# A fused attention and gated MLP kernel: fewer PSUM banks for the direct gelu tiles, and other places for the exps that VectorE computes

## The chip, the cores and the metric

The kernel runs on one core of one Trainium2 chip. The metric is the device time of one execution in microseconds; the time before is the median of four runs, 462.97 us (462.76 to 463.13). Engines are named as in the profile: PE is TensorE's matmul (PEld its weight load), DVE is VectorE, ACT is ScalarE, POOL is GpSimd, SP is the engine that issues most DMAs.

## What is computed

The reference normalises `x` (2048 rows of 448), sends the result through a 16-head attention with head size 28 and, beside it, through an MLP with gelu and silu, and combines both with `x`. Cut to what matters:

```
xn = layernorm(x)                                  # [2048, 448]
q, k, v = split(xn @ wqkv)                         # 16 heads of 28
o = softmax(q k^T / sqrt(28)) v                    # per head, 2048 x 2048 scores
s = o @ wo
h = gelu_tanh(xn @ w1 + b1)                        # [2048, 1792]
g = silu(h @ w2 + b2)                              # [2048, 448]
return x + s * g
```

## The kernel before

**Tiles.** Everything is done on transposed data. The 2048 rows are four chunks `c` of 512, the 16 heads four groups `g` of four. A score tile is 128 keys by 512 queries of one head; there are 4 x 4 blocks of 16 x 4 tiles, 1024 in all, numbered `m`. PE computes a tile from `kT` and `qT` with 32 active rows, so that up to four tiles of different heads run in the array at once. An exp follows (without a maximum; the norms of q and k that are folded into one row keep it in range), and PE multiplies the result by `vaug` and sums in the PSUM bank `acc` (PV, four heads side by side in columns).

**Who does the exps.** Most are done by ACT, in units of two or three tiles straight from PSUM (`p_exps`, L1276). The 33 quads of four tiles that `QUADS` lists are done by DVE instead: one pass from PSUM per tile, here called a head (`p_apass`, L1379), and then five passes over all four tiles in SBUF (`p_expq`, L1430 to L1437). So 132 tiles are DVE's, and 892 are ACT's.

**PSUM.** Of eight banks, `acc` holds the PV sum, six are the `ring`, and the last is `misc`. ACT's units alternate between ring banks 0 to 2 (three tiles) and banks 4 and 5 (two tiles). Ring bank 3 and `misc` are the side banks. All other products that need a bank, projections, w1 and w2 products, head tiles, normalisation and output products, take one from the list `banks` and give it back (`bank()` takes the one that came free first).

**The order of the work.** A planner in the kernel writes each engine's program. It runs small processes (generators) that yield tasks with a planned duration and a priority, or wait for a condition or a bank; it always takes the task that can start first, within 0.1 us the one with the lowest priority number. PE executes its program in order, and waits in it for semaphores of ACT and DVE. A head tile waits until it can join the pending ring score of other heads (`may_join`, `join`), for at most `WAIT`; during gelu it is issued alone at once (`in_gelu`). A quad may start when the scores have come to its first tile, during gelu up to `GLEAD` = 32 tiles earlier (`p_late`). Where the planned share of PE over 3.4 us falls under 85%, `p_busy` inserts fillers, three products with a zero matrix into `acc` (L903).

**Gelu.** The gelu of all 56 tiles of h (128 x 512 each) is done in one stretch, as ACT must load another table for it. 35 tiles were computed earlier and copied to SBUF by DVE (`p_f1`, L1070); ACT applies gelu to these in pieces of 5, 5, 4, 5, 5, 4, 5 and 2. Between the pieces come seven groups of three tiles which ACT reads directly from PSUM (`DIRECT`, `p_direct`, `p_gelu`, L1125). During this stretch the ring holds no scores: the direct groups use all six banks, in turns of three. For that, `p_take3` takes bank 3 from the list, from twelve tiles before `GM` until the last direct group is read, and DVE's heads have `misc` alone. The stretch begins with the first unit whose last tile is at or beyond `GM` = 582 (`gu` is its number). The score of unit `gu + 1` is issued when the last direct group is read.

**Where the exps' results lie.** ACT writes into 18 slots of `P`, before gelu also into 9 + 12 slots in the still unused parts of `h`, and after gelu into 15 slots of `xnT`, which is not read any more (`p_room`, `assign`; the profile's names for outputs are therefore P, h and xnT). `room_free` holds gelu's direct pieces until the slots in `h` are read by PV.

**After gelu** come the w2 products (`p_f2`, L1146), the silu of each chunk (a tanh on ACT, `p_silu`, L1161), the normalisation of each block (`p_epi`) and the output products (`p_out`, `p_last`).

Of the kernel before, what the change touches and what calls it, by code (L numbers as in the profile page):

```python
# [24 lines left out]
NRING = 6  # L25
NP = 18
# [1 line left out]
MTOT = NBLK * T * 4  # L28

GM = 64 * 9 + 6  # L30
QUADS = (17, 22, 24, 35, 36, 50, 55, 66, 75, 85, 89, 97, 106, 116, 118, 132, 139, 147, 148, 149, 151, 163, 173, 178, 186, 193, 201, 209, 216, 222, 225, 235, 242)
SM_SCALE = DH ** -0.5
LOG2E = 1.4426950408889634
EXP_A3, EXP_A2, EXP_LC = 0.16391228, 0.00783292, 1.1187538523466403
# [14 lines left out]


# [23 lines left out]
class _Kernel:  # L74
# [183 lines left out]
    def alloc(self):  # L258
# [3 lines left out]
        B = _Buf  # L262
# [104 lines left out]
        self.b_P += self.b_hf[2][5:14] + self.b_hf[3][0:12] + [B() for _ in range(16)]  # L367
        self.pon = [(0, NP)]
        self.b_nm = [[B(), B()] for _ in range(C)]
        self.b_selb = B()  # L370
# [13 lines left out]
    def schedule(self):  # L384
        K = self
# [695 lines left out]
    def t_f1(self, c, ft, bank, tok, k, prio=5):  # L1081
# [7 lines left out]
            return ins  # L1089
        return _Task(PE, f, [K.b_w1, K.b_w1pad, K.b_xnT[c][k]], [tok], 0.432, 0.17, prio)  # L1090

    def p_direct(self):
        K = self
        yield ("until", lambda: K.gu is not None and K.exp_u >= K.gu - 1 and K.bank3)
        s0 = 3 * ((K.gu - 1) % 2)
        for i, (c, f0) in enumerate(DIRECT):
            b0 = (s0 + 3 * i) % NRING
            yield ("until", lambda: K.exp_u >= K.gu - 1 + i if i < 2 else K.dir_read >= i - 1)
            for n in range(3):
                for k in range(2):  # L1100
                    yield K.t_f1(c, f0 + n, K.ring[:, b0 + n, :], K.b_ring[b0 + n], k, 3.5)
            K.dir_n += 1

    def p_gelu(self):
        K = self
        yield ("until", lambda: K.gu is not None and K.exp_u >= K.gu and K.n_f1 == len(SBT))
        left = [FT] * C
        s0 = 3 * ((K.gu - 1) % 2)
        for q, pc in enumerate(PIECES):
            if pc:  # L1110
                c, f0, n = pc
                src = K.h[:, c, 512 * f0:512 * (f0 + n)]
                rd = []
            else:
                i = K.dir_read
                yield ("until", lambda: K.dir_n > i and K.room_free())
                (c, f0), n = DIRECT[i], 3
                b0 = (s0 + 3 * i) % NRING
                src = K.ring[:, b0:b0 + 3, :].rearrange("p b n -> p (b n)")
                rd = K.b_ring[b0:b0 + 3]  # L1120
                for ft in range(f0, f0 + 3):
                    K.hf_free(c, ft)
            dst = K.h[:, c, 512 * f0:512 * (f0 + n)]
            left[c] -= n
            yield _Task(ACT, lambda eng, dst=dst, src=src: eng.activation(dst, src, ACTF.Gelu_apprx_tanh), rd,  # L1125
                        K.b_hf[c][f0:f0 + n] + ([K.b_h[c]] if left[c] == 0 else []),
                        0.4267 * n + (0.1 if pc else 0.06) + (1.3 if q == 0 else 0), 0.05, -1)
            if not pc:
                K.dir_read += 1
        K.prog[ACT].append(lambda eng: eng.preload_act_table_set("exp_and_others"))  # L1130
        K.tE[ACT] += 1.3
        for b in K.b_fsb + K.b_sig:
            b.w = K.b_w1.w
            b.r = list(K.b_w1.r) + [K.b_w1pad.w] + K.b_w1pad.r
        K.gelu_done = True

    def p_f2(self, c, t):
        K = self
        bank, tok = yield ("bank", lambda: K.b_h[c].tw is not None and K.ready([K.b_h[c], K.b_w2]) and K.dir_read == len(DIRECT) and (c < 2 or K.g_done[c - 2]))
        hv = K.h[:, c, :].rearrange("p (f n) -> p f n", n=512)  # L1140
        ps = bank[:, 0:D]
        for q in range(7):
            def f(eng, q=q):
                ins = None
                for ft in (2 * q, 2 * q + 1):
                    ins = eng.matmul(ps, hv[:, ft, t * 128:(t + 1) * 128], K.w2[:, ft, :],  # L1146
                                     start=(ft == 0), stop=(ft == FT - 1))
# [60 lines left out]
    def t_score(self, ms, bank_of, tok_of, prio):  # L1208
        K = self
        fl, rd = [], []  # L1210
# [22 lines left out]
    def p_scores(self):  # L1233
        K = self
        u = 0
        while K.next_m < MTOT:
# [1 line left out]
            if K.next_m >= MTOT:  # L1238
                break
            if K.gu is not None and u == K.gu + 1:  # L1240
                yield ("until", lambda: K.dir_read == len(DIRECT))
            b0 = 4 * (u % 2)
            n = 2 if b0 or K.next_m < 64 else 3
            if n == 3 and not K.taken:
# [99 lines left out]
        p["task"].dur, p["task"].rows = t.dur, t.rows  # L1344

    def in_gelu(self):
        return self.gu is not None and self.exp_u >= self.gu - 1 and self.dir_read < len(DIRECT)

    def p_late(self):
        K = self  # L1350
# [34 lines left out]
    def p_room(self):  # L1385
        K = self
        yield ("until", lambda: K.stg_done == 2)
        for ft in range(12):
# [5 lines left out]
        for b in K.b_P[NP + 21:]:  # L1394
            for x in K.b_xnT:
                for y in x:
                    b.r += y.r
        K.pon.append((NP + 21, 15))

    def room_free(self):  # L1400
        K = self
        return all(K.pv_done[m] for i, m in K.plast.items() if NP <= i < NP + 21)

    def assign(self, ms, b0):
        K = self
# [274 lines left out]
```

## Time and profile before

| | |
|---|---|
| median of 4 runs | 462.97 us |
| profiled execution | 463.12 us, of which the span from the first to the last instruction is 461.3 us |
| granted TensorE clock, mean | 0.996 |
| ACT busy | 448.1 us, 97% of the span |
| PE busy | 433.8 us, 94% |
| DVE busy | 368.2 us, 80% |
| POOL busy | 45.4 us, 10% |
| exps on ACT from the ring (L1276) | 363 instructions, 419.6 us (durations overlap) |
| direct gelus from the ring (L1125) | 7 instructions, mean 1457 ns |
| fillers on PE (L903) | 513 matmuls |

The profile shows one execution; its own time stands a little above the median. A row "busy" is the time in which the engine has at least one instruction in work. ACT overlaps the end of one instruction with the start of the next, so the distance from start to start (1.33 us for three tiles, 0.91 for two) is less than the duration in the groups. Idle time is put down to what ended it.

### The profile page before, as it was taken

The numbers are of one execution on the slowest core, as the hardware profiler recorded it, in microseconds if no ns is written. First come the engines' busy times: TensorE is split into PE (matmuls) and PEld (weight loads), VectorE is DVE, ScalarE is ACT, GpSimd is POOL, SyncE is SP. The second block draws the span as 40 slices with busy tenths as digits, with TensorE's granted clock in tenths as the row PEclk, the third lists the DMA queues.
The fourth block names the chain that finished last, engine by engine and source line by source line (L and its number), as shares of the span: only waits on it lengthen the run. The fifth ranks groups of instructions, "written<-read, shape, count | busy, mean of one in ns | idle before, by whom it ended". The sixth has DMA issues, their size and how long they took to land.

```text
span 461.3 us, 10748 instructions
## 1 busy us (share of the span) xinstructions
PE 433.8 (94%) x4509; PEld 169.1 (37%) x4543; DVE 368.2 (80%) x576; ACT 448.1 (97%) x407; POOL 45.4 (10%) x85
## 2 busy tenths in 40 slices
PE   6999899999999999999999999999999999999995
PEld 4533333333332233333333443233323344343552
DVE  7956898898887899968888577666877898996965
ACT  6999999999999999999999999999999999999994
POOL 7470000001010100000000000000000101101211
PEclk9999999999999999999999999999999999999998
DMA  8701000000000000000040000000000010200331
GB/s 266 269 2 37 2 1 0 1 2 3 2 1 1 1 0 3 2 1 2 1 141 0 1 3 0 2 2 1 0 1 1 1 41 2 35 9 1 43 43 41
DMA packets 8049, 11.17 MB, mean 24 GB/s; under 512 B 1697, under 2 KB 6993, under 8 KB 7954
## 3 DMA queue, kind: packets, MB, share of 16 engines
q1 hardware_dynamic: 6850, 8.43, 5.9%
q0 software_dynamic: 864, 1.38, 2.3%
q8 instruction: 36, 0.59, 0.5%
q10 hardware_dynamic: 288, 0.69, 0.4%
q14 instruction: 11, 0.09, 0.1%
HBM read 8.61 MB, written 3.21 MB: 26 GB/s over the span
## 4 chain that ended last, share of the span: by engine, by line
PE 48%; ACT 36%; issue 11%; DVE 2%; DMA 1%; SPq 0%; POOL 0%; ACTq 0%; DVEq 0%; POOLq 0%
ACT P L1276 18%; PE ring L1220 14%; ACT h L1276 10%; PE acc L1491 10%; ACT xnT L1276 6%; PE misc L1146 5%; PE ring L1146 4%; PE ring L1087 3%; PE acc L903 3%; PE misc L742 2%; PE misc L1087 2%; ACT h L1125 2%; PE ring L742 1%; DMA h<-in_A_wqkv_dram 1%; PE misc L1220 1%
## 5 line engine op out<-in xcount | busy, mean ns | idle before, releaser
L1276 ACT ACTIVATE P<-ring 128x1024 bf16<-128x1024 f32 (+1 forms) x194 | 221.8, 1260 | 1.8 <-PE misc L1220 0.8
L1220 PE MATMUL ring<-qT,kT 32*128 32x512 bf16 (+2 forms) x1082 | 142.6, 358 | 12.4 <-ACT P L1276 4.8
L1276 ACT ACTIVATE h<-ring 128x1024 bf16<-128x1024 f32 (+1 forms) x97 | 114.3, 1292 | 0.3 <-PE misc L1220 0.2
L1220 PEld LDWEIGHTS ring<-qT,kT 32*128 32x128 bf16 x1082 | 36.9, 91 | 133.3 <-ACT P L1276 57.5
L1276 ACT ACTIVATE xnT<-ring 128x1536 bf16<-128x1536 f32 (+1 forms) x72 | 83.5, 1269 | 0.0
L1491 PE MATMUL acc<-P,vaug 128*32 128x512 bf16 (+2 forms) x535 | 47.3, 358 | 0.0
L1561 POOL CAST rhi<-rc 128x16 bf16<-128x16 f32 x15 | 7.8, 523 | 359.2 <-DVE rc L1559 266.9
L903 PE MATMUL acc<-ident,zero 128*128 128x128 bf16 x513 | 41.4, 220 | 0.0
L1087 PE MATMUL ring<-xnT,w 128*128 128x512 bf16 x132 | 35.1, 381 | 1.5 <-issue 1.0
L903 PEld LDWEIGHTS acc<-ident,zero 128*128 128x128 bf16 x513 | 29.2, 98 | 17.6 <-issue 16.5
L1379 DVE TENSOR_SCALAR x_sb<-misc 128x512 uint16<-128x512 f32 x29 | 20.0, 689 | 13.0 <-PE misc L1220 12.9
L1146 PE MATMUL misc<-w,h 128*128 128x448 bf16 x112 | 27.2, 355 | 0.0
L1220 PE MATMUL misc<-qT,kT 32*128 32x512 bf16 (+1 forms) x70 | 26.0, 376 | 0.3 <-DVE qT L1578 0.3
L1146 PE MATMUL ring<-w,h 128*128 128x448 bf16 x112 | 26.0, 355 | 0.0
L1491 PE MATMUL acc<-h,vaug 128*32 128x512 bf16 x241 | 25.4, 384 | 0.0
L1087 PE MATMUL misc<-xnT,w 128*128 128x512 bf16 x70 | 20.0, 381 | 1.3 <-issue 0.5
L1491 PE MATMUL acc<-xnT,vaug 128*32 128x512 bf16 (+2 forms) x240 | 17.8, 330 | 0.4 <-ACT xnT L1276 0.4
L1491 PEld LDWEIGHTS acc<-P,vaug 128*32 128x32 bf16 x535 | 12.0, 95 | 14.7 <-issue 11.3
L1087 PEld LDWEIGHTS ring<-xnT,w 128*128 128x128 bf16 x144 | 11.3, 97 | 16.5 <-issue 5.3
L1379 DVE TENSOR_SCALAR x_sb<-ring 128x512 uint16<-128x512 f32 x19 | 13.0, 687 | 4.6 <-PE ring L1220 4.4
L1125 ACT ACTIVATE h<-h 128x2560 bf16<-128x2560 bf16 (+2 forms) x8 | 16.7, 2083 | 0.0
L1070 DVE CAST h<-misc 128x512 bf16<-128x512 f32 x20 | 13.7, 687 | 2.5 <-PE misc L1087 2.3
(270 smaller groups left out, 651.1 us busy)
## 6 DMA issues: line engine op xcount, KB each, us to landing
w<-in_B_w_dram SPq DMA_DIRECT2D x1, 1568.0 KB, 7.2
w<-in_B_w_dram SPq DMA_DIRECT2D x1, 1344.0 KB, 9.2
out_dram<-in_A_x_dram SPq DMA_DIRECT2D x3, 448.0 KB, 11.2
out_dram<-h POOLq DMA_DIRECT2D x6, 224.0 KB, 3.8
x_sb<-in_A_x_dram SPq DMA_DIRECT2D x2, 448.0 KB, 5.1
h<-in_A_wqkv_dram SPq DMA_DIRECT2D x3, 168.0 KB, 4.9
x_sb<-in_A_x_dram ACTq DMA_DIRECT2D x1, 448.0 KB, 5.3
h<-in_A_x_dram SPq DMA_DIRECT2D x1, 448.0 KB, 3.4
```

The source lines that it names most:

```text
L742: ins = eng.matmul(bank, w[:, kt, g * 128:(g + 1) * 128], K.xnT[:, kt, c * 512:(c + 1) * 512], start=(kt == 0), stop=(kt == KT - 1))
L903: ins = eng.matmul(K.acc[:, 0:128], K.zero[:, :], K.ident[:, :], start=False, stop=True, skip_group_check=True)
L1070: yield _Task(DVE, lambda eng: eng.tensor_copy(dst, bank), [tok], wr, 0.69, 0.0, 2)
L1087: ins = eng.matmul(bank, K.w1[:, kt, ft * 128:(ft + 1) * 128], K.xnT[:, kt, c * 512:(c + 1) * 512], start=(kt == 0), stop=(kt == KT - 1))
L1125: yield _Task(ACT, lambda eng, dst=dst, src=src: eng.activation(dst, src, ACTF.Gelu_apprx_tanh), rd, K.b_hf[c][f0:f0 + n] + ([K.b_h[c]] if ...
L1146: ins = eng.matmul(ps, hv[:, ft, t * 128:(t + 1) * 128], K.w2[:, ft, :], start=(ft == 0), stop=(ft == FT - 1))
L1220: return eng.matmul(dst, K.kT[32 * j:32 * j + 32, g, t * 128:(t + 1) * 128], K.qT[32 * j:32 * j + 32, g, c * 512 + q0:c * 512 + q0 + nq], ...
L1276: return eng.activation(reg[:, i0:i0 + n, :], K.ring[:, b0:b0 + n, :], ACTF.Exp, scale=SM_SCALE)
L1379: yield _Task(DVE, lambda eng: eng.tensor_scalar(K.unit[u][:, 512 * k:512 * k + 512].bitcast(dt.uint16), bank, SM_SCALE * LOG2E * 128.0, ( ...
L1491: return eng.matmul(K.acc[32 * j:32 * j + 32, q0:q0 + nq], K.vaug[:, t, 4 * g + j, :], ap[:, col:col + nq], tile_position=(0, 32 * j), sta ...
L1561: yield _Task(POOL, lambda eng: eng.tensor_copy(K.rhi[:, :], K.rc[:, :]), [K.b_rc], [K.b_rhl], 1.1, 0.0, 1)
```

## The change

The direct tiles of gelu no longer use all six ring banks. `directs()` forms eight groups (`ND`) in the ring's usual places, three tiles on banks 0 to 2 and two on banks 4 and 5 in turn, 20 tiles in all; the first group goes to the banks of unit `gu - 1`. Bank 3 is not taken from the list any more (`p_take3` is gone). 36 tiles go through SBUF now, in pieces of 5, 5, 4, 5, 5, 4, 4 and 4, each followed by a direct group, also the last. The slots for exps in `h` become 10 + 10 instead of 9 + 12. During gelu a quad may start up to 48 tiles early instead of 32. `QUADS` is another list of again 33 quads. The planner makes new orders for PE, DVE and ACT from all this.

```diff
-QUADS = (17, 22, 24, 35, 36, 50, 55, 66, 75, 85, 89, 97, 106, 116, 118, 132, 139, 147, 148, 149, 151, 163, 173, 178, 186, 193, 201, 209, 216, 222, 225, 235, 242)
+QUADS = (17, 22, 25, 35, 36, 50, 54, 65, 76, 84, 89, 99, 102, 116, 118, 132, 140, 142, 145, 152, 153, 162, 164, 179, 186, 194, 204, 210, 211, 214, 228, 233, 243)
...
-DIRECT = [(2, 5), (2, 8), (2, 11), (3, 0), (3, 3), (3, 6), (3, 9)]
+ND = 8
 PIECES = [(0, 0, 5), None, (0, 5, 5), None, (0, 10, 4), None, (1, 0, 5), None, (1, 5, 5), None, (1, 10, 4), None,
-          (2, 0, 5), None, (3, 12, 2)]
+          (2, 0, 4), None, (3, 10, 4), None]
...
-LEAD, WAIT, GLEAD = 0, 3.0, 32
+LEAD, WAIT, GLEAD = 0, 3.0, 48
...
-        self.pslots += [(hx(2, 5, 9), k) for k in range(9)] + [(hx(3, 0, 12), k) for k in range(12)]
+        self.pslots += [(hx(c, f, 10), k) for c, f in ((2, 4), (3, 0)) for k in range(10)]
...
-        K.spawn(K.p_take3(), 0)
...
+    def directs(self):
+        K = self
+        out, left = [], [[2, 4], [3, 0]]
+        for i in range(ND):
+            b0 = 4 * ((K.gu - 1 + i) % 2)
+            n = 2 if b0 else 3
+            c, f0 = left[i // (ND // 2)]
+            left[i // (ND // 2)][1] += n
+            out.append((c, f0, n, b0))
+        return out
...
     def p_direct(self):
         K = self
-        yield ("until", lambda: K.gu is not None and K.exp_u >= K.gu - 1 and K.bank3)
-        s0 = 3 * ((K.gu - 1) % 2)
-        for i, (c, f0) in enumerate(DIRECT):
-            b0 = (s0 + 3 * i) % NRING
+        yield ("until", lambda: K.gu is not None and K.exp_u >= K.gu - 1)
+        for i, (c, f0, nf, b0) in enumerate(K.directs()):
             yield ("until", lambda: K.exp_u >= K.gu - 1 + i if i < 2 else K.dir_read >= i - 1)
-            for n in range(3):
+            for n in range(nf):
...
-    def p_take3(self):
-        K = self
-        K.bank3 = False
-        yield ("until", lambda: K.next_m >= GM - 12 and any(t is K.b_ring[3] for _, t in K.banks))
-        e = K.banks.pop([t is K.b_ring[3] for _, t in K.banks].index(True))
-        K.bank3 = True
-        yield ("until", lambda: K.dir_read == len(DIRECT))
-        K.banks.append(e)
...
-        K.pon += [(NP, 9), (NP + 9, 12)]
+        K.pon += [(NP, 10), (NP + 10, 10)]
...
-        K.pon.append((NP + 21, 15))
+        K.pon.append((NP + 20, 15))
```

More of the change, by code (lines that the diff above doesn't have):

```diff
@@ L364, in alloc @@
         self.pslots = [(self.P[:, i0:i0 + n, :], k) for i0, n in ((0, NP),) for k in range(n)]
-        self.pslots += [(hx(2, 5, 9), k) for k in range(9)] + [(hx(3, 0, 12), k) for k in range(12)]
+        self.pslots += [(hx(c, f, 10), k) for c, f in ((2, 4), (3, 0)) for k in range(10)]
         self.pslots += [(self.xnT[:, :, :].rearrange("p k (c n) -> p (k c) n", n=512), k) for k in range(16)]
-        self.b_P += self.b_hf[2][5:14] + self.b_hf[3][0:12] + [B() for _ in range(16)]
+        self.b_P += self.b_hf[2][4:14] + self.b_hf[3][0:10] + [B() for _ in range(16)]
         self.pon = [(0, NP)]
@@ L1107, in p_gelu @@
         left = [FT] * C
-        s0 = 3 * ((K.gu - 1) % 2)
         for q, pc in enumerate(PIECES):
@@ L1116, in p_gelu @@
                 yield ("until", lambda: K.dir_n > i and K.room_free())
[L1117 to L1121, printed above, removed]
+                c, f0, n, b0 = K.directs()[i]
+                src = K.ring[:, b0:b0 + n, :].rearrange("p b n -> p (b n)")
+                rd = K.b_ring[b0:b0 + n]
+                for ft in range(f0, f0 + n):
                     K.hf_free(c, ft)
@@ L1138, in p_f2 @@
         K = self
-        bank, tok = yield ("bank", lambda: K.b_h[c].tw is not None and K.ready([K.b_h[c], K.b_w2]) and K.dir_read == len(DIRECT) and (c < 2 or K.g_done[c - 2]))
+        bank, tok = yield ("bank", lambda: K.b_h[c].tw is not None and K.ready([K.b_h[c], K.b_w2]) and K.dir_read == ND and (c < 2 or K.g_done[c - 2]))
         hv = K.h[:, c, :].rearrange("p (f n) -> p f n", n=512)
@@ L1240, in p_scores @@
             if K.gu is not None and u == K.gu + 1:
-                yield ("until", lambda: K.dir_read == len(DIRECT))
+                yield ("until", lambda: K.dir_read == ND)
             b0 = 4 * (u % 2)
@@ L1346, in in_gelu @@
     def in_gelu(self):
-        return self.gu is not None and self.exp_u >= self.gu - 1 and self.dir_read < len(DIRECT)
+        return self.gu is not None and self.exp_u >= self.gu - 1 and self.dir_read < ND
     def p_late(self):
@@ L1387, in p_room @@
         yield ("until", lambda: K.stg_done == 2)
-        for ft in range(12):
+        for ft in range(10):
             K.hf_free(3, ft)
-        K.pon += [(NP, 9), (NP + 9, 12)]
+        K.pon += [(NP, 10), (NP + 10, 10)]
         yield ("until", lambda: K.next_m >= GM - 24)
@@ L1393, in p_room @@
         yield ("until", lambda: K.gelu_done)
-        for b in K.b_P[NP + 21:]:
+        for b in K.b_P[NP + 20:]:
             for x in K.b_xnT:
@@ L1397, in p_room @@
                     b.r += y.r
-        K.pon.append((NP + 21, 15))
+        K.pon.append((NP + 20, 15))
     def room_free(self):
         K = self
-        return all(K.pv_done[m] for i, m in K.plast.items() if NP <= i < NP + 21)
+        return all(K.pv_done[m] for i, m in K.plast.items() if NP <= i < NP + 20)
     def assign(self, ms, b0):
```

## The prediction

> **What bounds the kernel now.** I read the page first, then the waits of ACT, then a table of stages, then single stretches of ACT's and PE's timelines, and at last the instruction orders of the two built programs side by side, engine by engine.
>
> ```profile
> span 461.3 us, 10748 instructions
> PE 433.8 (94%) x4509; PEld 169.1 (37%) x4543; DVE 368.2 (80%) x576; ACT 448.1 (97%) x407; POOL 45.4 (10%) x85
> PEclk9999999999999999999999999999999999999998
> ...
> ACT P L1276 <- PE misc L1220: 0.8, 1, 0.8
> ACT P L1276 <- PE ring L1220: 0.8, 2, 0.5
> ACT h L1276 <- PE misc L1220: 0.2, 1, 0.2
> ...
> 247.00:265.00 18.00, 17.60 (x104) 6.71 (x103) 12.22 (x17) 17.97 (x12) 0.00 (x0) 1.00 0.00 1
> 300.00:360.00 60.00, 59.61 (x515) 20.11 (x514) 42.90 (x59) 59.06 (x51) 1.62 (x4) 1.00 0.00 1
> 446.00:462.00 16.00, 9.61 (x220) 5.12 (x217) 9.54 (x18) 9.06 (x9) 2.11 (x2) 0.86 0.18 43
> ```
>
> ACT is busy 448.1 of 461.3 us. Of the 13.2 idle, 5.2 lie in the first 15 us (loads, layernorm) and 6.9 behind the last exp, in a fixed chain (last PV product, reciprocal, output projection, output DMA). Between 15 and 446 us ACT idles only some 1.5 us, and all of it on scores from PE. The columns of the stage rows are PE, PEld, DVE, ACT, POOL: in gelu (247 to 265) DVE has 5.8 us to spare and PE almost nothing.
>
> So the time is ACT's work plus the places where PE brings a score late. The largest such place:
>
> ```profile
> 315.85 4.62 ACT L1276 ACTIVATE P<-ring 128x1536 bf16<-128x1536 f32 x4
> 321.28 2.37 ACT L1276 ACTIVATE P<-ring 128x1536 bf16<-128x1536 f32 x2 [0.81 <-PE misc L1220]
> ...
> 318.45 0.39 PE L1220 MATMUL ring<-qT,kT 32*128 32x512 bf16 x2
> 318.77 0.93 PE L1146 MATMUL ring<-w,h 128*128 128x448 bf16 x4
> 319.64 0.61 PE L1491 MATMUL acc<-xnT,vaug 128*32 128x512 bf16 x7
> 320.83 0.39 PE L1220 MATMUL ring<-qT,kT 32*128 32x512 bf16 x3
> ```
>
> Between the starts of two successive ring scores PE does four w2 products and five rounds of PV: 2.38 us. The ring holds two units (banks 0 to 2 and banks 4, 5), and two exps together take 2.24 us (1.33 + 0.91), so whatever PE puts between two scores beyond about 1.6 us (2.24 less a score's 0.31 and the hand-overs) is taken from ACT. That threshold I use below.
>
> **The change part by part.**
>
> *ACT's own work.* Both orders have 363 exp units, 197 of two tiles and 166 of three, and 33 quads on VectorE: no exp leaves ACT. Only gelu differs. Start to start:
>
> ```profile
> 250.49 2.34 ACT L1125 ACTIVATE h<-h 128x2560 bf16<-128x2560 bf16 x1
> 252.73 1.43 ACT L1125 ACTIVATE h<-ring 128x1536 bf16<-128x1536 f32 x1
> 254.06 2.33 ACT L1125 ACTIVATE h<-h 128x2560 bf16<-128x2560 bf16 x1
> 257.62 1.91 ACT L1125 ACTIVATE h<-h 128x2048 bf16<-128x2048 bf16 x1
> 259.42 1.45 ACT L1125 ACTIVATE h<-ring 128x1536 bf16<-128x1536 f32 x1
> ```
>
> Five tiles from SBUF take 2.24, four 1.80, three from the ring 1.33. A gelu of two ring tiles is not in the trace; two thirds of 1.33 bounds it below (0.89), half of a four-tile piece plus 0.05 above (0.95); I take the two-tile exp's pitch, 0.91, since gelu and exp have the same 1.33 at three tiles. Before: 5 x 2.24 + 2 x 1.80 + 7 x 1.33 + 1.11 for the last piece = 25.2. After: 4 x 2.24 + 4 x 1.80 + 4 x 1.33 + 3 x 0.91 + 1.08 = 25.3. Cost: +0.1.
>
> *Head and tail.* The PE order is equal up to its 350th instruction, ACT's up to its 46th (about 45 us): 0. Behind the last exp both orders have the same instructions, with misc and a ring bank swapped: 0. DMA queues and GpSimd: the same instructions in the same order on both, so 0. DVE gets one copy more (one more w1 tile goes through SBUF, 0.69 us): hidden, DVE is 80% busy and ACT does not wait for it; if that cover were gone it would cost its 0.69.
>
> *New places: where PE stands between scores.* I went through PE's order in both programs, adding trace durations between successive ring scores: 0.216 per 512-column matmul (30 of them in 6.65), 0.19 per w2 product, 0.22 per round of four PV products, 0.06 per filler, 0.1 for each change between row, column and full tiling (scores start at 318.45, the w2 product 0.32 later). For the place above this gives 2.33 against 2.38 seen. Beyond the equal head, the places over 1.6 us with no silu or table load just ahead (these hand PE their own 1.6 or 1.3 us of ACT time) are, by exp unit counted from 0:
> before: 62 (1.69), 64 (1.90), 68, 116 (1.91), 118 (1.79), 122, 140, 178, 198, 227, 250 (2.33), 274, 294;
> after: 62, 64, 68, 122, 178, 204 and 284 (each at most 1.90).
> The ones at silus are 2.70, 2.28 and 2.59 before, 2.06, 1.91, 2.28 and 2.06 after. So the places at 250 and 116 are gone (there PE now carries 1.37 and 0.84). They are the waits of 0.81 and 0.20 us: -1.0. Waits under about 0.17 us do not show as idle, because one ACT row overlaps the next; from the starts of all exps, ACT loses 6.1 us against the pitches 0.906 and 1.333, 4.8 of it behind the equal head. Units 118, 198 and 274 lose 0.12, 0.23 and 0.24 in this way and go; 204 and 284 come, at some 0.15 each. Net -0.3, between -1.0 (the bursts at silus lose less, too) and +0.8 (other places pay as much as these did).
>
> *Gelu stage.* The six-bank groups of three become groups on banks 0 to 2 and 4, 5. Bank 3 is meant for the heads. In PE's order it isn't: one head uses it at the start, then the last query projection (`p_q(3, 3)`) takes bank 3 and holds it until gelu is over: its products have priority 5, behind the direct tiles' 3.5, and stand just behind the last of these. So 13 of 14 single scores go through misc alone, against 9 before, each with two changes of tiling:
>
> ```profile
> 266.43 0.39 PE L1220 MATMUL misc<-qT,kT 32*128 32x512 bf16 x1
> 266.74 1.04 PE L1087 MATMUL ring<-xnT,w 128*128 128x512 bf16 x4
> 267.71 0.38 PE L1220 MATMUL misc<-qT,kT 32*128 32x512 bf16 x1
> ```
>
> A head period of 1.28 holds four w1 products (0.86), so a head costs PE 0.42. From the release of the first group to the score behind gelu, PE has 40 pairs of w1 products (17.2), 13 heads (5.4), PV and small products with their changes (4.3): about 27 us of the 28.6 that ACT needs. Fillers vanish there. Going through it in order with the releases, groups 0 to 5 are ready 0.6 to 1.3 us early, group 6 is some 0.25 late, group 7 just in time. DVE has 14 evictions (0.62 pitch), seven 1.22 products and eleven 0.7 steps, some 27 us: full too. Behind a head that waits for VectorE queue all w1 products of the next groups, and ACT waits for those. Bound: 0 (if PE gains 0.25 elsewhere) to +3 (below); I take +0.25, nearest to the rows. A gain is excluded: ACT has no wait in gelu to lose. The last group is now the last piece; its 0.91 and the table load's 1.28 cover the next score (0.32): 0.
>
> *Fewer fillers.* 513 filler matmuls become 444. The trace shows clock 1.00 in every stage up to 446 us. [...] By the row it is 0, and I take 0: the fillers still stand wherever the planned PE share of 3.4 us drops below 85%, and they vanish where real work stands.
>
> *Sum* on the profiled execution (463.12 = span 461.3 + 1.8 around it): +0.1 - 1.0 - 0.3 + 0.25 = -0.95, so 462.17 there. The median of the four runs, 462.97, lies 0.15 under the profiled one: 462.0.
>
> **The rivals.**
> *Silent waits go too* (0.15). Of the 4.8 us lost behind the head another 1.0 goes, since PE's bursts of 2.3 to 2.7 us shrink to 2.1 to 2.3: 461.0. For it: fewer bursts. Against: silent losses stood also where no burst was.
> *Given back* (0.15). The new places bring joint scores that wait for an eviction elsewhere; -1.0 becomes about 0: 462.9. For it: both place lists fill ACT to 99.7%, so there is little to win. Against: no place above 1.91 is left outside silus.
> *Slower: misc as the only head bank in gelu* (0.15). Eleven heads stand ahead of group 6. If each costs PE only 0.17 more than my 0.42, because PE waits for a DVE that is full, group 6 comes 1.9 later, and the total passes 463.9; at 0.25 more it is 462.0 + 2.7 = 464.7, the bound above. For it: DVE and PE both have about 1.5 us spare in 28. Against: DVE idles 0.6 us ahead of most heads at 266 to 271 us, so the heads there waited for PE, not PE for them.
> [...]
> *That the change doesn't do what it says*: bank 3 is left free but not used by the heads, as shown; it is part of the likeliest case.
>
> **How the numbers follow.** Likeliest (0.52): 462.0, own range 461.2 to 462.8. A difference of 0.2%, 0.93 us, is about what a measurement of this kernel can tell from no change: below 462.04 is faster, above 463.90 slower. The likeliest case lies at that edge, 0.29 of it faster, 0.23 same. Faster: 0.29 + 0.15 = 0.44. Same: 0.23 + 0.14 of the third case = 0.37. Slower: 0.15 + 0.03 + 0.01 = 0.19. Range 461.0 to 463.8, which leaves out the far ends of the second and fourth case.
>
> **What would show it.** Right: no ACT wait near 0.8 on a misc or ring score between 300 and 340 us; ACT idle under 1.0 us between 15 us and the last exp outside gelu; a wait of 0 to 0.5 us before the seventh or eighth direct gelu (groups 6 and 7); clock 1.00; 6.9 us behind the last exp. Wrong: waits over 1 us at direct gelus (the fourth case), a clock under 1.00 in the middle, or new waits of ACT on scores at units outside my list.

## The result and the profile after

| | before | after |
|---|---|---|
| median of all executions | 462.94 us (60) | 462.24 us (42) |
| shortest | 462.73 us | 462.14 us |
| profiled execution: span | 461.3 us | 460.4 us |
| mean granted TensorE clock | 0.996 | 0.999 |
| ACT busy | 448.1 us | 448.4 us |
| fillers on PE | 513 matmuls | 444 matmuls |

The ratio of the mean times is 0.9988, with a 95% interval from 0.9983 to 0.9992. The kernel became 0.70 us (0.15%) shorter by the medians, 0.57 us by the means and 0.59 us by the shortest executions. All of these lie within the 0.2% that the prediction had set as the bound of what can be told from no change, with the whole interval on the side of faster.

The head of the page, and four of the stage rows (window, length, then PE, PEld, DVE, ACT and POOL with their busy us and instructions, granted clock, DMA share, GB/s), of the kernel after:

```profile
span 460.4 us, 10597 instructions
PE 434.0 (94%) x4443; PEld 164.8 (36%) x4474; DVE 368.1 (80%) x577; ACT 448.4 (97%) x408; POOL 42.6 (9%) x85
PEclk9999999999999999999999999999999999999999
...
247.00:265.00 18.00, 17.68 (x104) 6.00 (x106) 16.14 (x22) 18.00 (x12) 0.00 (x0) 1.00 0.00 1
265.00:300.00 35.00, 34.37 (x282) 11.38 (x281) 20.85 (x30) 34.97 (x31) 0.75 (x2) 1.00 0.01 2
300.00:360.00 60.00, 59.66 (x521) 19.85 (x524) 44.05 (x60) 59.86 (x52) 1.17 (x4) 1.00 0.00 1
446.00:462.00 16.00, 8.74 (x188) 4.60 (x184) 9.07 (x18) 8.36 (x8) 2.11 (x2) 0.91 0.09 30
```

Between 300 and 360 us ACT is busy 59.86 us instead of 59.06: this is the wait of 0.8 us that the prediction showed. During gelu (247 to 265) DVE now has 16.14 busy us instead of 12.22. That work was brought forward: in the next stage DVE has 20.85, where the kernel before had 24.52. ACT has no wait for DVE in either stage, so nothing shows that this move brings anything by itself.

The waits of ACT for PE (us in total, times, the longest), all rows from 0.3 us on the ring:

```profile
ACT P L1273 <- PE ring L1217: 0.8, 2, 0.5
ACT xnT L828 <- PE ring L816: 0.3, 1, 0.3
ACT qsq L867 <- PE ring L932: 0.3, 1, 0.3
```

Both rows on `misc` scores are gone. The row of 0.8 on `ring` scores is the one of before, in the part of the order that both kernels share. At the place that had the wait (exp unit 250) the timelines of ACT and PE now read:

```profile
313.33 6.08 ACT L1273 ACTIVATE P<-ring 128x1536 bf16<-128x1536 f32 x5
319.29 1.04 ACT L1273 ACTIVATE xnT<-ring 128x1024 bf16<-128x1024 f32 x1
...
317.43 0.39 PE L1217 MATMUL ring<-qT,kT 32*128 32x512 bf16 x3
317.75 0.55 PE L1152 MATMUL misc<-w,h 128*128 128x448 bf16 x2
318.23 0.39 PE L1217 MATMUL ring<-qT,kT 32*128 32x512 bf16 x3
318.56 0.93 PE L1152 MATMUL misc<-w,h 128*128 128x448 bf16 x4
319.51 0.61 PE L1217 MATMUL ring<-qT,kT 32*128 32x512 bf16 x4
```

From score to score PE takes 0.80 and 1.28 us, with two or four w2 products between them and no PV, and ACT runs through.

**What the wait rows do not show.** ACT overlaps the end of one row with the start of the next, so a score that is late by less than some 0.17 us leaves no idle time (before, a row of `P` of three tiles takes 1.506 us in the mean and the next can start 1.333 us behind its start; 1.076 and 0.906 for two). I therefore took the distance from the start of each exp to the start of ACT's next instruction, less the pitch of its size (0.906 us for two tiles, 1.333 for three), and summed it by exp unit, each under the unit that starts late. Here and in all that follows this is called the excess. That it is made by late scores can be read from the traces too: of the exps that start over 0.1 us late behind another exp (28 before, 30 after), 25 in each trace start within 0.07 us of the end of a score on PE; for the exps that are in time the median of this distance is 0.32 us.

| exp units (counted from 0) | before | after | largest single ones, before; after |
|---|---|---|---|
| 0 to 59 | 1.38 | 1.38 | the part that both share |
| 60 to 149 | 1.84 | 1.76 | 116: 0.39; 146: 0.28, 122: 0.22 |
| 150 to 239 | 1.32 | 1.17 | 213: 0.29, 227: 0.29; 204: 0.26 |
| 240 to 279 | 2.13 | 1.32 | 250: 0.94; 276: 0.23 |
| 280 to 362 | 1.14 | 1.43 | 302: 0.20; 314: 0.28 |
| sum | 7.81 | 7.06 | |
| gelu stage, from one table load to the other | 26.47 | 26.60 | |

The two places of the prediction lose 1.33 us in the kernel before (0.94 + 0.39), and neither as much as 0.07 after. All the rest went from 6.48 to 7.06, so a net 0.58 us was lost anew. With 0.13 more in gelu the sum is -1.33 + 0.58 + 0.13 = -0.62 us. From the start of the first exp to that of the last, the traces differ by 0.59 us (440.31 and 439.72).

### The profile page after: what moved, and what is told of

Same layout as the page of the kernel before. It is cut to its first block, busy times and chain, and to the rows that moved or that the text cites. A ratio compares the mean times of both kernels' runs of the same rounds, so it can differ in the third digit from the quotient of the medians.

```text
span 460.4 us, 10597 instructions
## 1 busy us (share of the span) xinstructions
PE 434.0 (94%) x4443; PEld 164.8 (36%) x4474; DVE 368.1 (80%) x577; ACT 448.4 (97%) x408; POOL 42.6 (9%) x85
## 3 DMA queue, kind: packets, MB, share of 16 engines
q0 software_dynamic: 864, 1.38, 2.3%
## 4 chain that ended last, share of the span: by engine, by line
PE 51%; ACT 35%; issue 10%; DVE 2%; DMA 1%; POOL 0%; ACTq 0%; DVEq 0%; POOLq 0%
ACT P L1273 16%; PE ring L1217 14%; ACT h L1273 12%; PE acc L1488 10%; ACT xnT L1273 6%; PE ring L1086 5%; PE ring L1152 4%; PE misc L1152 4%; PE acc L902 3%; PE misc L1086 2%; PE misc L741 1%; PE misc L1217 1%; PE ring L741 1%; PE misc L1585 1%; PE ring L1585 1%
## 5 line engine op out<-in xcount | busy, mean ns | idle before, releaser
L1488 PE MATMUL acc<-P,vaug 128*32 128x512 bf16 (+2 forms) x537 | 50.6, 357 | 0.4 <-ACT P L1273 0.4
L1086 PE MATMUL ring<-xnT,w 128*128 128x512 bf16 x143 | 38.2, 381 | 1.3 <-issue 1.0
L902 PE MATMUL acc<-ident,zero 128*128 128x128 bf16 x444 | 36.3, 220 | 0.0
L902 PEld LDWEIGHTS acc<-ident,zero 128*128 128x128 bf16 x444 | 25.3, 98 | 15.0 <-issue 13.6
L1217 PE MATMUL misc<-qT,kT 32*128 32x512 bf16 (+1 forms) x80 | 29.6, 374 | 0.0
L1376 DVE TENSOR_SCALAR x_sb<-misc 128x512 uint16<-128x512 f32 x34 | 23.4, 687 | 7.6 <-PE misc L1217 7.0
L1488 PE MATMUL acc<-xnT,vaug 128*32 128x512 bf16 (+2 forms) x236 | 21.2, 331 | 0.0
L1546 DVE CAST E_sb<-acc 128x512 bf16<-128x512 f32 x15 | 10.4, 691 | 10.6 <-PE acc L1488 10.5
L1131 ACT ACTIVATE h<-h 128x2560 bf16<-128x2560 bf16 (+1 forms) x8 | 17.0, 2130 | 0.0
L1376 DVE TENSOR_SCALAR kT<-ring 128x512 uint16<-128x512 f32 x18 | 12.4, 686 | 5.6 <-PE ring L1217 5.6
```

What stands on the lines that cost most here:

```text
L902: ins = eng.matmul(K.acc[:, 0:128], K.zero[:, :], K.ident[:, :], start=False, stop=True, skip_group_check=True)
L1086: ins = eng.matmul(bank, K.w1[:, kt, ft * 128:(ft + 1) * 128], K.xnT[:, kt, c * 512:(c + 1) * 512], start=(kt == 0), stop=(kt == KT - 1))
L1217: return eng.matmul(dst, K.kT[32 * j:32 * j + 32, g, t * 128:(t + 1) * 128], K.qT[32 * j:32 * j + 32, g, c * 512 + q0:c * 512 + q0 + nq], ...
L1376: yield _Task(DVE, lambda eng: eng.tensor_scalar(K.unit[u][:, 512 * k:512 * k + 512].bitcast(dt.uint16), bank, SM_SCALE * LOG2E * 128.0, ( ...
L1488: return eng.matmul(K.acc[32 * j:32 * j + 32, q0:q0 + nq], K.vaug[:, t, 4 * g + j, :], ap[:, col:col + nq], tile_position=(0, 32 * j), sta ...
L1546: yield _Task(DVE, lambda eng: eng.tensor_copy(E, K.acc[:, :]), [K.b_acc], [tE], 0.7, 0.0, 0)
```

## The experiments

The theory (A in what follows): the gain is ACT's, and it comes from the places of the quads, in that no long stretch of PE stands between two scores at units 250 and 116; the five banks and the freed bank 3 bring nothing. The rival (B): the freed bank brings it, by giving VectorE's heads a second bank in gelu. A third: the smaller number of fillers matters, to either side. From e5 on, each expectation gives the letters a meaning of its own.

**e1: the banks alone.** The kernel after, with the list of places of the kernel before.

```diff
-QUADS = (17, 22, 25, 35, 36, 50, 54, 65, 76, 84, 89, 99, 102, 116, 118, 132, 140, 142, 145, 152, 153, 162, 164, 179, 186, 194, 204, 210, 211, 214, 228, 233, 243)
+QUADS = (17, 22, 24, 35, 36, 50, 55, 66, 75, 85, 89, 97, 106, 116, 118, 132, 139, 147, 148, 149, 151, 163, 173, 178, 186, 193, 201, 209, 216, 222, 225, 235, 242)
```

> The changed kernel with the old list of quads: the change of banks alone. Theory A (the time is ACT's work plus the scores that PE brings late; the places must fit the order): slower than before. By the threshold of 1.6 us the PE order has stretches of 2.06, 1.91, 2.27 and 4.13 us at units 228, 230, 242 and 263 and more behind them; the excess adds up to some 4 us against 1.5 before: about 465.4 us, with ACT idle of 2 to 4 us between 280 and 350 us. Theory B (the two side banks left to the heads in gelu bring the gain): at most 462.3 us, as the changed kernel, since this part is all there.

Measured: 467.38 us, ratio 1.0095 [1.0081, 1.0108], slower than before. ACT's longest wait, and the two longest in its timeline:

```profile
ACT P L1273 <- PE acc L1488: 3.1, 1, 3.1
...
275.24 1.45 ACT L1131 ACTIVATE h<-ring 128x1536 bf16<-128x1536 f32 x1 [0.83 <-PE ring L1086]
...
340.24 2.37 ACT L1273 ACTIVATE P<-ring 128x1024 bf16<-128x1024 f32 x2 [3.15 <-PE acc L1488]
```

The second is an exp that waits for its slot in `P`, until PE's PV rounds that end at 340.1 have read it; these stand in PE's order behind six w2 products. The first is a direct gelu that comes 0.83 us late, in the same way as the prediction had it for group 6, but larger. So the bank layout with the old list loses 4.4 us against the kernel before, 2.0 us more than the expectation had; a wait for a slot was not in its sum.

**e2: the places alone.** The kernel before, with the list of the kernel after (the diff of e1 the other way round, in the kernel before).

> The kernel before with the new list of quads: the change of places alone. Theory A: slower, about 467 us: PE's order has a stretch of 5.98 us ahead of unit 240 (the excess over 1.6 us is 4.4) and others of 2.8 and 3.55 us near silus; ACT idle of 4 to 5 us near unit 238 to 240. Theory B: no gain and no loss from places, about 462.9 us. Theory C (the new places are better wherever they stand): about 462.2 us.

Measured: 471.47 us, ratio 1.0184 [1.0171, 1.0198].

```profile
ACT xnT L1276 <- PE acc L1491: 5.1, 1, 5.1
ACT P L1276 <- PE acc L1491: 1.9, 1, 1.9
```

This is the same kind of wait, for slots, and longer: the loss is 8.5 us, where the expectation had some 4. The wait of 1.9 us stands behind the last silu. Neither half of the change stands by itself: a list is fitted to one layout, and with another layout the planner meets the slots at other times. From e1 and e2 alone one can't say which half holds the gain. That needs a list that is fitted to the old banks.

**e3: six banks with a list fitted to them.** The kernel before, so also with its 9 + 12 slots and its lead of 32 tiles; only its list differs, in 13 of 33 places.

```diff
-QUADS = (17, 22, 24, 35, 36, 50, 55, 66, 75, 85, 89, 97, 106, 116, 118, 132, 139, 147, 148, 149, 151, 163, 173, 178, 186, 193, 201, 209, 216, 222, 225, 235, 242)
+QUADS = (17, 21, 23, 35, 37, 50, 55, 65, 75, 85, 90, 97, 106, 116, 118, 132, 139, 146, 148, 149, 151, 161, 165, 179, 186, 194, 201, 209, 216, 222, 227, 233, 243)
```

> The kernel before, six banks in gelu as it was, with a third list of 33 quads that was fitted to it: units 0 to about 213 keep their stretches of PE (1.91 us at unit 116 too), but the one of 2.33 us at unit 250 is 1.75 and the one of 2.59 at 272 is gone. Theory A: the wait of 0.81 us at unit 250 goes without any change of banks, the one of 0.20 stays: 462.0 to 462.3 us, ratio about 0.9985. Theory B: 462.9 us, as the banks are the old ones.

Measured: 462.3 us, ratio 0.9987 [0.9978, 0.9995], as for the kernel after (0.9988). Its timeline at unit 250 has no idle time (the excess there is 0.25 us instead of 0.94); the wait at unit 116 is still there:

```profile
308.83 6.90 ACT L1276 ACTIVATE xnT<-ring 128x1536 bf16<-128x1536 f32 x6
315.73 6.19 ACT L1276 ACTIVATE P<-ring 128x1536 bf16<-128x1536 f32 x5
...
138.96 1.45 ACT L1276 ACTIVATE h<-ring 128x1536 bf16<-128x1536 f32 x1 [0.20 <-PE misc L1220]
```

So a gain of the same size can be had without the new banks, slots and lead. Most of the wait at unit 250 belonged to the list, not to the layout.

**e4: no fillers at all.** The kernel after without `p_busy`.

```diff
-        K.spawn(K.p_busy(), 100)
```

> The changed kernel without any filler matmul (444 less; they write zeros to a sum, so the result keeps its meaning). If the granted clock depends on them: the mean clock falls under 0.99, with stretches under 1.00 where the fillers were dense (360 to 450 us), and the time rises by 1 to 10 us. If PE's real work is enough to hold the clock: clock 0.99 or more and 461.8 to 462.3 us. I lean to the first, since a third of PE's time from 360 us on would be empty.

Measured: 471.98 us, ratio 1.0197 [1.0164, 1.0231]. The clock row of the page, the stages from 300 us on, and the waits:

```profile
PEclk9999999999999999999999999999999967977799
...
300.00:360.00 60.00, 59.30 (x511) 19.55 (x510) 44.05 (x60) 59.86 (x52) 1.16 (x4) 1.00 0.01 2
360.00:400.00 40.00, 32.39 (x310) 8.90 (x308) 31.91 (x46) 37.59 (x34) 1.62 (x4) 0.83 0.04 12
400.00:446.00 46.00, 38.43 (x397) 11.61 (x395) 33.59 (x48) 41.13 (x36) 5.39 (x8) 0.79 0.16 21
...
ACT P L1272 <- PE ring L1216: 6.2, 10, 1.2
```

Behind 360 us, where the w2 products run out (in the kernel after, the last stands at 370 us) and mostly scores and PV are left for PE, the granted clock falls to 0.83 and 0.79 in the mean, and ACT waits for scores. In this execution the clock ahead of 360 us stayed at 1.00 with no filler at all. I read from it that the early fillers could go; e6 tests that.

**e5: bank 3 free for the heads.** In the kernel after, the last query projection may not take a bank before gelu's last direct tile is read.

```diff
-... and ((g, c) == (0, 1) or K.boot()))
+... and ((g, c) == (0, 1) or K.boot()) and ((g, c) != (3, 3) or K.gelu_done))
```

> The kernel after, with one condition more: the last query projection p_q(3, 3) may not take a bank before the last direct gelu is read, so bank 3 is free for VectorE's heads all through gelu. Theory A (the held bank cost only what group 6 of gelu came late, 0.11 us, and what comes behind gelu gives that back): group 6 starts 1.80 us after the start of its piece instead of 1.91, the query projection then stands behind gelu, where ACT's exps pay about 0.2 us for it; total 462.2 to 462.4, no difference from the kernel after (462.24). Theory B (single heads that share misc cost PE and VectorE time in gelu, and the quads that start there come later for it): the whole gelu stage frees 0.5 us or more of VectorE and PE, total 461.7 or less.

Measured: 462.19 us, ratio 0.9983 [0.9975, 0.9992]; no difference from the kernel after. PE's timelines, the kernel after first, then e5:

```profile
270.14 0.59 PE L1086 MATMUL ring<-xnT,w 128*128 128x512 bf16 x2
270.57 0.59 PE L741 MATMUL ring<-xnT,wq 128*128 128x512 bf16 x2
```

```profile
248.02 0.38 PE L1217 MATMUL ring<-qT,kT 32*128 32x512 bf16 x1
248.02 0.39 PE L1217 MATMUL misc<-qT,kT 32*128 32x512 bf16 x1
249.31 0.39 PE L1217 MATMUL ring<-qT,kT 32*128 32x512 bf16 x1
```

In the kernel after, the projection's products on bank 3 come right behind the last direct tile, as the prediction read it from the order, and the heads from 247 us until then are all on `misc`. In e5 heads stand on both banks. The direct gelu of group 6 then starts on time. Here are the piece ahead of it and the gelu, in the kernel after, and then in e5:

```profile
265.82 1.94 ACT L1131 ACTIVATE h<-h 128x2048 bf16<-128x2048 bf16 x1
267.73 1.45 ACT L1131 ACTIVATE h<-ring 128x1536 bf16<-128x1536 f32 x1
```

```profile
265.96 1.94 ACT L1131 ACTIVATE h<-h 128x2048 bf16<-128x2048 bf16 x1
267.76 1.48 ACT L1131 ACTIVATE h<-ring 128x1536 bf16<-128x1536 f32 x1
```

From start to start this is 1.91 us and 1.80. So the held bank costs 0.11 us, and behind gelu unit 216 loses 0.19 that it does not lose in the kernel after. Theory A, to the number: freeing bank 3 is worth nothing here, with this list.

**e6: fillers only behind gelu.** The kernel after with one condition changed in `p_busy`; 252 filler matmuls are left of 444.

```diff
-        yield ("until", lambda: K.pv_m >= 0)
+        yield ("until", lambda: K.next_m >= 640)
```

> The kernel after, with fillers only from score tile 640 on (behind gelu). The run without any filler kept a clock of 1.00 up to 360 us and fell to 0.8 behind. Theory A (the fillers ahead of gelu hold up nothing and keep up nothing): clock 1.00 in all stages, total within 0.3 us of the kernel after, 461.9 to 462.3. Theory B (the early fillers stand in front of scores and cost ACT): ACT's losses in units 34 to 100 fall from 1.33 to about 1.16 us as in the run without fillers, total 462.0. [...]

Measured: median 463.81 us, ratio 1.001 [0.9994, 1.0025]. The median hides what happened. Five of twelve executions took 461.97 to 462.16 us at a mean granted clock of 0.997 to 0.998, and seven took 463.6 to 465.24 at 0.988 to 0.994. The profiled one was among the five: clock 1.00 in every stage up to 446 us, and an excess 0.17 us less than in the kernel after (units 34 to 99), as theory B had it. So theory B fits five executions. The other seven are 1.5 to 3.1 us longer at a lower mean clock, which neither theory had in it; no trace of them was kept, so where their clock fell is not shown. One trace can't show a fault that comes in part of the executions; e4's trace, on which I built this experiment, had the same defect.

**e7: the program of e5 with its own list.** 11 places differ from the list after.

```diff
-QUADS = (17, 22, 25, 35, 36, 50, 54, 65, 76, 84, 89, 99, 102, 116, 118, 132, 140, 142, 145, 152, 153, 162, 164, 179, 186, 194, 204, 210, 211, 214, 228, 233, 243)
+QUADS = (17, 22, 25, 35, 37, 50, 54, 65, 76, 84, 88, 99, 103, 116, 118, 132, 138, 139, 145, 151, 158, 163, 165, 179, 186, 194, 200, 210, 211, 220, 228, 233, 243)
```

> The kernel of e5 with a list of 33 places fitted to it anew (11 of them moved, by 1 to 6 tiles). Its planner ends 0.28 us earlier than that of e5 (453.49 against 453.77) since the losses at units 146 to 350 that it sees become fewer. Theory A (what the planner sees reaches the chip): 461.9 to 462.1, and 0.2 to 0.4 less than e5. Theory B (the silent losses of ACT, which the planner does not see, decide among such lists): anything from 461.8 to 462.7, with the sum of ACT's excess over its pitches, not the planner's end, in step with the time.

Measured: 461.78 us, ratio 0.9977 [0.9968, 0.9985], the fastest of all, 0.4 us under e5. Units 280 to 319 lose 0.48 us instead of 0.96.

**e8: the program of e6 with its own list**, 12 places from the list after.

> The kernel of e6 with a list of 33 places fitted to it anew; the planner ends 0.11 us earlier than that of e6 (453.47 against 453.58) and 0.21 earlier than that of the kernel after. Theory A (what the planner sees reaches the chip): 461.8 to 462.0, the fastest of all. Theory B (silent losses decide): anything from 461.8 to 462.7, in step with ACT's excess over its pitches in the trace.

Measured: 464.17 us, ratio 1.003 [1.0018, 1.0042]: all its executions are above 463.9 us. Both theories failed, since neither had the clock in it. This trace shows it, in windows of 1 us and in ACT's timeline, then PE's:

```profile
47.00:48.00 1.00, 0.76 (x8) 0.20 (x7) 1.00 (x3) 1.00 (x3) 0.00 (x0) 1.00 0.00 0
48.00:49.00 1.00, 0.61 (x11) 0.26 (x7) 0.76 (x2) 1.00 (x2) 0.00 (x0) 1.00 0.00 0
49.00:50.00 1.00, 0.43 (x4) 0.12 (x4) 0.52 (x2) 1.00 (x2) 0.33 (x2) 1.00 0.00 0
50.00:51.00 1.00, 1.00 (x5) 0.31 (x4) 0.69 (x1) 1.00 (x2) 0.08 (x1) 0.83 0.00 0
51.00:52.00 1.00, 1.00 (x5) 0.13 (x4) 0.99 (x2) 0.78 (x1) 0.00 (x0) 0.50 0.00 0
52.00:53.00 1.00, 1.00 (x5) 0.40 (x4) 0.91 (x2) 0.91 (x1) 0.00 (x0) 0.50 0.00 0
53.00:54.00 1.00, 1.00 (x6) 0.10 (x3) 0.10 (x1) 0.11 (x1) 0.00 (x0) 0.50 0.00 0
54.00:55.00 1.00, 1.00 (x14) 0.22 (x11) 0.59 (x1) 0.65 (x1) 0.00 (x0) 0.97 0.00 0
...
52.09 1.02 ACT L1273 ACTIVATE P<-ring 128x1024 bf16<-128x1024 f32 x1 [0.31 <-PE ring L1217]
54.35 5.97 ACT L1273 ACTIVATE h<-ring 128x1536 bf16<-128x1536 f32 x5 [1.24 <-PE ring L1217]
...
51.98 1.89 PE L741 MATMUL misc<-xnT,wk 128*128 128x512 bf16 x4
```

The last row is PE's timeline. The same four products read so in the kernel after:

```profile
50.93 1.03 PE L741 MATMUL misc<-xnT,wk 128*128 128x512 bf16 x4
```

For three microseconds PE is busy 0.76, 0.61 and 0.43 of each, never idle for as much as 0.8 us at a time. Then the clock is 0.50 for about 3.4 us, an estimate from 0.83, 0.50 and 0.97 (0.34 + 3 + 0.06 us, if the rest of the first and the last window has 1.00). The four products take 1.89 us instead of 1.03, and ACT waits 0.31 and 1.24 us for the scores behind them. PE's busy share alone does not tell when the clock falls. The profiled execution of e6 has the same share at the same place and kept its clock:

```profile
46.50:49.50 3.00, 1.79 (x19) 0.58 (x18) 2.25 (x5) 3.00 (x4) 0.35 (x2) 1.00 0.00 0
```

In the trace of e4 PE is busy only 2.47 of the 4 us from 46 to 50 (2.80 in e8), and the clock stays at 1.00 there and up to 62 us.

**e9: e8 with the fillers from the beginning.** The list of e8, 447 filler matmuls instead of 255, nothing else.

> The places of e8, with the fillers from the beginning again; nothing else differs. In e8 the clock fell to 0.50 from about 50 to 54 us, behind 3 us in which PE was busy 1.8 us, and ACT lost 1.55 us there. Theory A (the missing early fillers made that): clock 1.00 in every stage from 15 to 446 us, units 34 to 60 lose 0.49 us again instead of 1.96, total 462.0 to 462.4, and no run of 464 or more. Theory B (the place list does it: other work of PE around 50 us): the clock falls there again and the total stays at 463.8 to 464.3.

Measured: 462.31 us, ratio 0.9988 [0.9979, 0.9996]; the longest of eleven executions took 462.83. Units 34 to 59 lose 0.49 again instead of 1.96. Theory A: the early fillers are worth 1.9 us with this list (464.17 - 462.31), of which these units show 1.47. The two ran on different chips, but that does not explain it: on the chip of e8, the 21 executions of e5 and e7, which have the early fillers, show no mean clock under 0.995, and the six of e8 none over 0.994.

**e10: a second list for the program of e7**, 17 of its 33 places are not in e7's.

> The program of e7 with a second list fitted to it (18 of 33 places differ from the list of e7); its planner ends 0.04 us later than that of e7 (453.53 against 453.49). Theory A (what the planner sees reaches the chip, so that lists planned alike run alike): 461.7 to 461.9. Theory B (silent losses that the planner does not see decide): a difference of 0.2 us or more to e7 (461.78), in step with ACT's excess over its pitches (e7: 6.55 us).

Measured: 462.04 us, ratio 0.9983 [0.9974, 0.9992]. Theory A wanted 461.9 at most; the 0.26 us to e7 (0.19 by the shortest executions) are what B calls for. The figure of 6.55 us for e7 in the expectation left out one exp, the one ahead of gelu's first table load, which ACT doesn't overlap with it (in the kernel after the exps ahead of it end at 245.27 us and the load starts at 245.30). With it the excess is 6.68 us in e7 and 6.83 in e10, so 0.15 of the difference is seen there.

**Eight kernels that kept their clock, side by side.** The sum is excess plus gelu stage, from one trace each, whose stage rows have clock 1.00 up to 446 us. For e6, too, the shortest execution is one of those with a mean clock of 0.997 to 0.998.

| | excess + gelu | shortest execution | difference | median |
|---|---|---|---|---|
| before | 7.81 + 26.47 = 34.28 | 462.73 | 428.45 | 462.94 |
| after | 7.06 + 26.60 = 33.66 | 462.14 | 428.48 | 462.24 |
| e3 | 6.93 + 26.47 = 33.40 | 461.85 | 428.45 | 462.30 |
| e5 | 7.15 + 26.53 = 33.68 | 462.13 | 428.45 | 462.19 |
| e6 | 6.92 + 26.60 = 33.52 | 461.97 | 428.45 | 463.81 |
| e7 | 6.68 + 26.52 = 33.20 | 461.66 | 428.46 | 461.78 |
| e9 | 6.91 + 26.61 = 33.52 | 462.01 | 428.49 | 462.31 |
| e10 | 6.83 + 26.53 = 33.36 | 461.85 | 428.49 | 462.04 |

The difference is the same within 0.04 us in all eight. Part of this is bookkeeping: the pitches and the silus are alike, so within each trace the sum gives the length from the first exp to the last, whatever causes it. What the table adds is that the shortest executions follow this length alone. The sum counts waits behind an exp only. e1 and e2 kept their clock too (0.999 and 0.998 in the mean of the profiled executions); e1 fits (467.20 less 38.8 is 428.4), and e2 is 2.0 us off (471.23 less 40.8 is 430.5), as the exp behind its last silu waits 1.91 us.

The traces are not those of the shortest executions: the profiled ones took 0.39 us more (before) and 0.45 us more (e5). This arises ahead of the first exp (12.57 to 12.82 us in the eight traces) and behind the start of the last (8.03 to 8.23). The two with 8.23 are before and e5. Before, the clock fell to 0.50 at 457.6 us, while the last output product ran, which took 0.54 us instead of 0.36; in e5 the clock from 446 to 462 us is 0.81 in the mean (0.86 before, 0.91 after). Here is that product before, and then after:

```profile
457.53 0.54 PE L1588 MATMUL ring<-wo,qT 128*128 128x448 bf16 x1 [1.61 <-DVE qT L1540]
456.84 0.36 PE L1585 MATMUL misc<-wo,qT 128*128 128x448 bf16 x1 [1.62 <-DVE qT L1537]
```

By the shortest executions e3, with six banks, lies 0.3 us below the kernel after, and e7, with bank 3 free for the heads, 0.2 us below e3. Two lists for one program differ by as much (e7 and e10, 0.19), so differences of this size do not rank the layouts. The medians scatter more: executions of one kernel differ by up to 1.1 us (462.14 to 463.27 after).

## Why the prediction was right, and where it was not

Predicted were 462.0 us and a range from 461.0 to 463.8; measured 462.24. The likeliest case was the right one, and its mechanism, PE's stretches at units 250 and 116, was too; that the sum came as near as 0.24 us is in part luck, since two terms were off in opposite directions. "Faster by over 0.2%" had the higher chance (0.44 against 0.37), and "within 0.2%" is what came. By its steps:

- *ACT's own work, +0.1*: right. The direct gelu of two tiles takes 0.90 to 0.91 from start to start where I took 0.91, and three take 1.33.
- *The waits at units 250 and 116, -1.0*: right in place and cause. They gave back 1.33, because each also held a silent part (0.94 against the 0.81 shown, 0.39 against 0.20).
- *Silent waits, -0.3*: this term failed in its sign. Without those two units, the excess went from 6.48 to 7.06, so it rose by 0.58, towards the far end of my +0.8. The places that I had named behaved as I had said (198 and 274 lost 0.23 and 0.24 and went; 204 and 284 came with 0.26 and 0.18). But the list held only single stretches of PE over 1.6 us. Units 146, 276 and 314 (0.28, 0.23 and 0.28) are not on it, and a dozen of 0.1 to 0.15 neither. The threshold was the fault: at 314 two shorter stretches in a row add up. In the kernel after, PE's scores and ACT's exps there are:

```profile
395.20 0.39 PE L1217 MATMUL ring<-qT,kT 32*128 32x512 bf16 x3
396.38 0.39 PE L1217 MATMUL ring<-qT,kT 32*128 32x512 bf16 x2
397.73 0.39 PE L1217 MATMUL ring<-qT,kT 32*128 32x512 bf16 x3
...
395.63 2.42 ACT L1273 ACTIVATE xnT<-ring 128x1536 bf16<-128x1536 f32 x2
398.17 1.45 ACT L1273 ACTIVATE P<-ring 128x1536 bf16<-128x1536 f32 x1
```

The stretches are 1.18 and 1.35 us, both under 1.6, and together 2.53, more than the 2.24 of two exps; ACT starts its third exp 2.54 us after its first. Unit 146 is alike (1.29 and 1.40), and 276 stands just behind a silu's long stretch (2.32 and 1.56). My figure of ACT's losses in the kernel before, 6.1 us in all and 4.8 behind the equal head, was too small: with every exp set against the pitch of its own size they are 7.8 and 6.4.
- *Gelu stage, group 6 late by 0.25*: the mechanism was right, the size 0.11; group 7 was in time, and the stage grew by 0.13. e5 shows the cause: with bank 3 free, the lateness is gone.
- *Bank 3 held by the query projection through gelu*: right, read from the instruction order. e5 puts its price at 0.1 us in gelu.
- *Fewer fillers, 0*: right for this change, clock 1.00 in every stage up to 446 us. The chance of slower counts a term of 0.03 that no run shows. What the runs showed in its place is a loss in e8, with fewer fillers still: about 3.4 us at half clock by the estimate above, and 1.55 us of ACT's time, though PE was not idle ahead of it for more than 0.77 us at a time. The row of the clock in one execution, on which I rested the 0, would not have shown such a loss: the planner goes on inserting fillers wherever its share falls below 85%, and e9, which has the early fillers and the list of e8, had no mean clock under 0.995. e6, which leaves out the early ones of this kernel, had a mean clock of 0.988 to 0.994 in seven of twelve executions.
- *Head and tail, 0*: right for the kernel. 0.59 us of the 0.9 between the spans lie between the first and the last exp. The other 0.3 lies in the head (0.11) and in the tail (0.19, the product at half clock above), in instructions whose order is the same; executions of one kernel differ by more. The 6.9 us behind the last exp counted 0.7 us past the end of the span: ACT idles 6.3 us there before and 6.1 after, and 1.8 between 15 us and the last exp, not 1.5. The sum does not use these.
- *The sum, -0.95*: measured -0.62 by excess and gelu, -0.59 by the shortest executions, and -0.70 by the medians. Two errors met: -1.3 for waits became -0.75, and +0.35 for gelu became +0.13. What ACT idles from 15 us to the last exp fell from 1.77 to 0.90 us, gelu included; the sign that the prediction had named was under 1.0.

Of the rivals, *silent waits go too* did not come in this kernel; e7 reaches 461.78 by just this way. A clock under 1.00 in the middle did not come either; e8 had it, at 464.2 us. *Given back* came in part: 0.58 of 1.33. *Misc as the only head bank* did not come: before four of the 13 heads on `misc` DVE idles until PE has written them, and ACT lost no more there than the 0.11. One of the four:

```profile
259.79 0.69 DVE L1376 TENSOR_SCALAR x_sb<-misc 128x512 uint16<-128x512 f32 x1 [0.41 <-PE misc L1217]
```

*That the change doesn't do what it says* was so for bank 3, and it did not matter (e5).

## What to carry to other kernels

When one engine is busy 97% of the time, measure its loss from start to start of its instructions; the idle column misses every wait that is shorter than the overlap of two rows (0.17 us), here most of the loss (in the kernel after 7.06 us of excess, 0.90 of idle time). Look for late scores over two successive stretches of PE, as the ring holds two units, and not over single ones. When a change brings a new layout and new fitted places together, fit places to the old layout too before the layout gets the credit: here both halves alone lost 4.4 and 8.5 us, and the old layout with its own list did as well as the new one. What fillers do for TensorE's clock cannot be judged from one trace: the profiled execution of e6 took 462.16 us at a mean clock of 0.998, seven others 463.6 to 465.24 at 0.988 to 0.994. Compare the spread of the times and their mean clocks as well.

## What the runs showed of the hardware that was not expected

- The clock fell to one half without any long idle stretch of PE: in e8 it came after 3 us in which PE was 60% busy, in pieces of at most 0.77 us idle, and lasted about 3.4 us by the estimate above. The same share did not do it elsewhere: the profiled execution of e6 had PE busy 1.79 of 3 us (46.5 to 49.5) and kept 1.00, as did e4 with 2.47 of the 4 us from 46 to 50 (2.80 in e8). Seven others of e6 lost 1.5 to 3.1 us. So a busy share read from one trace does not tell whether the clock will hold, and what else decides stays open. The lossy executions of e6 were not traced; that they fell at the same place is argued from e8 and e9, not shown.
- With no filler at all (e4) the clock stayed at 1.00 from 40 to 360 us, with PE busy 53.27 of the 60 us from 40 to 100. It was 0.83 in the mean from 360 to 400 us, with PE busy 32.39 of 40, and 0.79 from 400 to 446, with PE busy 38.43 of 46.
- The shortest times of eight kernels, out of 462 us, follow the sum of ACT's excess and the gelu stage to 0.04 us. So the waits that no idle column shows counted here with their length: e10 has 0.15 us more of excess than e7, and its shortest execution is 0.19 us longer.
